# Half-size loads, nine slots, and one value unit split unevenly over the DMA engines, in a one-token attention block

## The chip, the cores and the metric

The kernel runs on one core of a Trainium2 chip. The metric is the device time of one execution in microseconds; lower is better. The kernel before takes 393.2 us (median of three runs, 392.14 to 393.55).

## The reference

One token (x, 1024 numbers) goes through two blocks, and a scalar gate mixes them. Block A is attention against a long cache: 32 query heads share 4 key/value groups, the cache holds 65,536 positions of 128 numbers for each group. Block B is a gated mixer for a sequence of one.

```
q = (x @ wq) as 32 heads of 128
scores = q . k_cache / sqrt(128)            # 32 x 65536, 8 heads use one group
a = softmax(scores) @ v_cache @ wo          # 4096 -> 1024
z = gelu(x @ w_in)                          # 1024 -> 3584 = z1 (1792), z2 (1792)
b = (z1 * (w_sp * layernorm(z2) + b_sp)) @ w_out
g = sigmoid(sum(x * gate_w))
out = g * a + (1 - g) * b
```

All inputs are bf16. Keys and values are 67.1 MB each, wq and wo 8.4 MB each, w_in 7.3 MB, w_out 3.7 MB: 162 MB that are read once.

## The kernel before

Every operation is given to a recorder (`R.op`, short `P`) with its engine, what it reads and what it writes. The recorder derives the waits between engines from that and emits each engine's instructions in the order in which they were given. A transfer has a semaphore of its own name that rises by 16, one for each DMA engine that has finished its part.

The caches are worked through in units of 8192 positions (`UK`): 8 units a group, 32 in all, each 2 MB of keys and 2 MB of values. In a unit, partition p holds 64 consecutive positions, 16 KB. Two neighbouring units are loaded by one transfer (`pair`, `kv`), 32 KB a partition.

All large inputs go through one ring in SBUF of `NS` = 5 slots of 32 KB a partition (`SLOT` = 16384 elements). `load` writes the order down in a list, `stream`; `issue(upto)` gives SP the transfers in this order (L338), round robin over the slots. The first five are issued at once (`issue(NS)`). After that, `done(key)` is called where PE has used a unit; when the last unit of a load is done, the load five places later is issued. SP waits in order. The order of the list is: query weights (two loads), then key pairs with the mixer's input weights (`win`, two loads) and output weights (`wout`, one) between them, then key pairs and value pairs in turn with values nine units behind, then the attention's output weights (`wo`, four loads of 16 KB a partition).

Four small transfers are issued by ACT at the very start (`small`, L261): x and the gate's weights, as 128 partitions with two runs of four numbers each, and two scalars that are broadcast.

PE's order is: the gate's sum (L371, which waits for x and the gate's weights), the queries (L386), and then step by step. A step has up to one key unit n and one value unit n - 9. For the key unit PE transposes 64 tiles of 128x128 in eight batches (`k_piece`, L411); ACT (L416) and DVE (L419) bring each batch from PSUM to one of `NKTS` = 6 buffers; PE multiplies them with the queries (`s_piece`, L433) and DVE takes the scores to one of `NSC` = 10 buffers with their maximum (L438). For the value unit ACT takes exponentials (L459), PE turns them (L466), DVE copies (L469) and PE multiplies them with the values (`pv_piece`, L478). Values start nine units late because the group's maximum must be known. The mixer's two matrices are worked in between: `win_piece` (L526) after key units 1 and 3, two parts each, `wout_piece` (L574) after key unit 6. At the end PE multiplies the attention output with `wo` (L621), DVE adds both blocks (L627), and SP stores 2 KB (L630).

## Time and profile before

| What | Value |
|---|---|
| Median of three runs | 393.2 us |
| The profiled execution's own time | 393.2 us |
| Its span in the profile | 390.4 us |
| Busy share PE / PE weight load / DVE / ACT | 70% / 50% / 41% / 32% |
| Bulk DMA queue q1, share of 16 engines | 97.1%, 162.01 MB |
| Rate over the span | 415 GB/s read |
| Granted TensorE clock, mean | 0.85 |
| Landing of x and of the gate's weights, after issue | 22.4 and 39.2 us |
| Median from issue to landing, key and value pairs | 30.2 and 31.7 us |

How to read it. The page cuts the span into 40 slices of 9.8 us and gives for each the busy tenths of every engine, of the 16 DMA engines together (DMA) and their rate (GB/s). Queue q1 carries the transfers that SP issues, q10 those of ACT; q8 and q14 carry instructions and tables that the engines' sequencers fetch. The chain that ended last goes back from the last instruction to what released it. An answer by windows has one line for each stretch: start and end, length, busy time and number of instructions of PE, PE weight load, DVE, ACT and POOL, granted clock, DMA share, GB/s. The trace also keeps every DMA packet (queue, bytes, start, duration, but not which of the 16 engines carried it) and the time of every semaphore step of a transfer.

### The profile page before, as it was taken

To read this page: it belongs to the slowest core of one execution; us is meant where nothing else is said; L and a number is where in the kernel's file an instruction comes from. 1 tells how busy PE (TensorE), PEld (TensorE's weight loads), DVE (VectorE), ACT (ScalarE), POOL (GpSimd) and SP (SyncE) were. 2 spreads that over 40 slices of the span, in tenths; PEclk is the share of its full clock that TensorE was granted. 3 is DMA by queue.
4 is the path that set the end of the run, shared out by engine and by line. 5 is a ranking of instruction groups with operands and counts; after the bars stand their busy time and mean duration, and the time that the engine had idled before them with its cause. 6 is when DMAs were issued, how large, how long until landed. Compare 5 with 4: busy or idle time off the path is not lost.

```text
span 390.4 us, 8502 instructions
## 1 busy us (share of the span) xinstructions
PE 274.1 (70%) x3902; PEld 194.6 (50%) x3902; DVE 160.2 (41%) x347; ACT 124.4 (32%) x171; POOL 1.5 (0%) x8
## 2 busy tenths in 40 slices
PE   0000699996999899976787596957974959574552
PEld 0000678885776676745565474645743736221121
DVE  2000043435666666644664263536742636410020
ACT  1000033332556555551355151613551425231000
POOL 1000000000000000000000000000000000000000
PEclk9999998685999999996899598968995989856555
DMA  8999999999999999999999999999999999999992
GB/s 322 430 430 437 418 412 441 426 428 425 411 405 431 433 426 431 428 431 428 427 431 428 428 431 430 425 435 435 428 431 433 428 426 431 433 431 421 416 415 96
DMA packets 6778, 162.54 MB, mean 416 GB/s; under 512 B 1492, under 2 KB 1496, under 8 KB 1496
## 3 DMA queue, kind: packets, MB, share of 16 engines
q1 hardware_dynamic: 5912, 162.01, 97.1%
q8 instruction: 30, 0.49, 0.5%
q10 hardware_dynamic: 832, 0.00, 0.1%
q14 instruction: 4, 0.03, 0.0%
HBM read 162.01 MB, written 0.00 MB: 415 GB/s over the span
## 4 chain that ended last, share of the span: by engine, by line
DMA 55%; PE 36%; DVE 6%; issue 1%; ACT 1%; ACTq 0%; DVEq 0%
DMA arena<-in_A_k_cache_dram 31%; PE pb L411 18%; DMA arena<-in_gate_w_dram 10%; DMA arena<-in_A_v_cache_dram 8%; PE pb L433 6%; DMA arena<-in_A_wo_dram 6%; PE pb L526 3%; DVE arena L419 3%; PE pb L478 3%; PE pb L386 2%; DVE arena L438 2%; PE pb L466 1%; ACT arena L416 0%; PE pb L621 0%; PE pb L574 0%
## 5 line engine op out<-in xcount | busy, mean ns | idle before, releaser
L411 PE MATMUL pb<-arena 128*128 128x128 bf16 x2048 | 153.6, 235 | 31.7 <-DMA arena<-in_A_k_cache_dram 31.7
L411 PEld LDWEIGHTS pb<-arena 128*128 128x128 bf16 x2048 | 131.9, 106 | 60.1 <-DMA arena<-in_A_k_cache_dram 34.7
L419 DVE COPY arena<-pb 128x1024 bf16<-128x1024 bf16 x160 | 108.3, 689 | 111.2 <-PE pb L411 110.2
L416 ACT ACTIVATE arena<-pb 128x1024 bf16<-128x1024 bf16 x96 | 98.0, 1021 | 162.2 <-PE pb L411 162.2
L433 PE MATMUL pb<-arena 128*32 128x512 bf16 x512 | 55.0, 420 | 6.1 <-DVE arena L438 4.2
L478 PE MATMUL pb<-arena 128*32 128x512 bf16 x512 | 39.9, 440 | 14.5 <-DMA arena<-in_A_v_cache_dram 10.5
L371 PE MATMUL pb<-arena 128*128 128x1 f32 x2 | 0.6, 362 | 41.0 <-DVE arena L370 41.0
L478 PEld LDWEIGHTS pb<-arena 128*32 128x32 bf16 x512 | 14.0, 104 | 28.5 <-issue 13.5
L459 ACT ACTIVATE arena<-arena 128x512 bf16<-128x512 f32 x32 | 22.8, 713 | 14.3 <-PE pb L466 12.6
L469 DVE COPY arena<-pb 128x512 bf16<-128x512 bf16 x32 | 13.6, 424 | 28.4 <-PE pb L466 28.4
L433 PEld LDWEIGHTS pb<-arena 128*32 128x32 bf16 x512 | 13.3, 93 | 22.9 <-DVE arena L438 7.7
L438 DVE TENSOR_SCALAR_CACHE_REDUCE arena<-pb 128x512 f32<-128x512 f32 x32 | 21.8, 682 | 2.8 <-PE pb L433 2.8
L371 PEld LDWEIGHTS pb<-arena 128*128 128x128 f32 x2 | 0.5, 313 | 41.0 <-DVE arena L370 41.0
L369 DVE TENSOR_TENSOR arena<-arena 128x8 f32<-128x8 bf16 x1 | 0.2, 168 | 37.2 <-DMA arena<-in_gate_w_dram 37.2
L466 PE MATMUL pb<-arena 128*128 128x128 bf16 x128 | 14.8, 248 | 0.0
L466 PEld LDWEIGHTS pb<-arena 128*128 128x128 bf16 x128 | 8.7, 109 | 11.4 <-issue 10.6
L526 PEld LDWEIGHTS pb<-arena 128*128 128x128 bf16 x224 | 13.6, 158 | 0.5 <-issue 0.5
L526 PE MATMUL pb<-arena 128*128 128x1 bf16 x224 | 13.8, 198 | 0.0
L373 ACT ACTIVATE arena<-pb 128x1 f32<-128x1 f32 x1 | 0.2, 171 | 37.0 <-PE pb L371 37.0
L621 PE MATMUL pb<-arena 128*1 128x256 bf16 x128 | 6.5, 379 | 6.8 <-DMA arena<-in_A_wo_dram 6.8
L386 PE MATMUL pb<-arena 128*128 128x1 bf16 x256 | 7.1, 165 | 2.1 <-issue 2.1
L621 PEld LDWEIGHTS pb<-arena 128*1 128x1 bf16 x128 | 3.6, 108 | 9.4 <-issue 4.4
(78 smaller groups left out, 59.7 us busy)
## 6 DMA issues: line engine op xcount, KB each, us to landing
arena<-in_A_k_cache_dram SPq DMA_DIRECT2D x16, 4096.0 KB, 30.2
arena<-in_A_v_cache_dram SPq DMA_DIRECT2D x16, 4096.0 KB, 31.7
arena<-in_A_wq_dram SPq DMA_DIRECT2D x2, 4096.0 KB, 17.4
arena<-in_A_wo_dram SPq DMA_DIRECT2D x4, 2048.0 KB, 30.1
arena<-in_B_w_in_dram SPq DMA_DIRECT2D x2, 3584.0 KB, 28.0
arena<-in_B_w_out_dram SPq DMA_DIRECT2D x1, 3584.0 KB, 17.3
arena<-in_A_x_dram ACTq DMA_DIRECT2D x1, 2.0 KB, 22.4
arena<-in_gate_w_dram ACTq DMA_DIRECT2D x1, 2.0 KB, 39.2
```

The source lines that it names most:

```text
L386: ins = e.matmul(pf(OB)[:, h:h + 1], sl[:, WQ_N * k + 128 * h:WQ_N * k + 128 * (h + 1)], xT[:, 2 * i + k:2 * i + k + 1], start=(i == 0 and ...
L411: ins = e.transpose(pbf(pb)[:, 128 * t:128 * (t + 1)], sl[:, 128 * (8 * b + t):128 * (8 * b + t + 1)], idb)
L416: P("ACT", lambda e, i=i, pb=pb: e.activation(ktb(i), pbf(pb), ACTF.Copy), w=[("kt", i % NKTS), B(pb)])
L419: P("DVE", lambda e, i=i, pb=pb: e.tensor_copy(ktb(i), pbf(pb)), w=[("kt", i % NKTS), B(pb)])
L433: ins = e.matmul(pf(SCB)[32 * cg:32 * (cg + 1), :], qpad[:, 128 * g + 32 * j:128 * g + 32 * (j + 1)], src, start=(j == 0), stop=(j == 3), ...
L438: P("DVE", lambda e: e.tensor_scalar(scs(n), pf(SCB), 0.0, None, op0=ALU.add, op1=ALU.max, accum_out=maxc[:, n:n + 1]), w=[("sc", n % NSC) ...
L459: P("ACT", lambda e: e.activation(psb(n), scs(n), ACTF.Exp, bias=gcol(g, K_NB), scale=SCALE, accum_out=lp[:, n:n + 1]), r=[("sc", n % NSC) ...
L466: ins = e.transpose(pbf(PTB)[:, 128 * xi:128 * (xi + 1)], psb(n)[:, 128 * xi:128 * (xi + 1)], idb)
L469: P("DVE", lambda e: e.tensor_copy(ptsb(n), pbf(PTB)[:, 0:512]), w=[("ptsb", n % 2), B(PTB)])
L478: ins = e.matmul(pf(OB)[32 * cg:32 * (cg + 1), :], ptsb(n)[:, 128 * xi + 32 * cg:128 * xi + 32 * (cg + 1)], vw(sl, 128 * (4 * cg + xi), [[ ...
L526: ins = e.matmul(pf(MB)[:, z:z + 1], vw(sl, c0, [[FC, 128]]), xT[:, 2 * i + k:2 * i + k + 1], start=(i == 0 and k == 0 and z == 0), stop=( ...
L621: ins = e.matmul(pf(FB)[32 * q:32 * q + 1, 0:QW], ovec[:, 8 * i + c:8 * i + c + 1], sl[:, DO * c + QW * q:DO * c + QW * (q + 1)], start=(i ...
```

## The change

- Every large load is one unit: 2 MB of keys, values, query weights or output weights, 14 KB a partition for `win` and `wout`. The ring has nine slots of 16 KB a partition in place of five of 32 KB, and a load is issued when the one nine places before it is done.
- `win` and `wout` come in four and two loads; their parts are worked after key units 0, 1, 2, 3 and 5, 7. The hidden numbers are placed so that PE's weight reads in `win_piece` step by 7 elements rather than 14. The rows of the query and mixer weights that a partition holds change with it, and so x and the gate's weights come as four runs of two numbers for each partition.
- `NKTS` is 8 and `NSC` is 12.
- One value unit, number 16 (`BAL`), is loaded by two transfers. The first takes partitions 0 to 79; its source is described as 8 groups of 10 rows, which spreads it over 8 DMA engines. The second takes partitions 80 to 127 in the usual way, over all 16, three rows each. The slot's semaphore rises by 32 for it.

## The prediction

> **What bounds the kernel now.** I read the page's slices first, then the DMA queues, the chain that ended last, and last the raw DMA records of the trace.

> ```profile
> span 390.4 us, 8502 instructions
> ...
> PE 274.1 (70%) x3902; PEld 194.6 (50%) x3902; DVE 160.2 (41%) x347; ACT 124.4 (32%) x171; POOL 1.5 (0%) x8
> ...
> DMA  8999999999999999999999999999999999999992
> GB/s 322 430 430 437 418 412 441 426 428 425 411 405 431 433 426 431 428 431 428 427 431 428 428 431 430 425 435 435 428 431 433 428 426 431 433 431 421 416 415 96
> ...
> q1 hardware_dynamic: 5912, 162.01, 97.1%
> q8 instruction: 30, 0.49, 0.5%
> q10 hardware_dynamic: 832, 0.00, 0.1%
> q14 instruction: 4, 0.03, 0.0%
> ```

> No compute engine is above 70%; the sixteen DMA engines are busy from the first slice to the last but one, 97.1% of the span with the bulk queue alone. So the time is the start, the bytes at the DMA rate, and a tail. The chain in order of time shows the tail and one place near the front where the DMA was not the limit:

> ```profile
> 1.21 39.23 DMA arena<-in_gate_w_dram
> 40.96 0.59 PE pb L371 x2
> ...
> 361.59 24.22 DMA arena<-in_A_wo_dram
> 385.95 1.91 PE pb L621 x32
> 387.88 0.42 DVE arena L627
> ```

> PE does nothing before the gate row lands at 40.4, then is behind until about 153. That costs time only if a slot of the ring comes free too late. It does once, in the stretches from 106 to 112:

> ```profile
> 104.00:106.00 2.00, 2.00 (x31) 1.44 (x32) 1.20 (x2) 0.97 (x2) 0.00 (x0) 1.00 1.08 459
> 106.00:108.00 2.00, 2.00 (x37) 1.56 (x34) 1.08 (x2) 1.45 (x2) 0.00 (x0) 1.00 0.95 328
> 108.00:110.00 2.00, 1.79 (x27) 1.16 (x27) 2.00 (x5) 1.02 (x1) 0.00 (x0) 1.00 0.87 344
> 110.00:112.00 2.00, 2.00 (x34) 1.67 (x34) 0.92 (x3) 1.00 (x1) 0.00 (x0) 1.00 0.83 360
> 112.00:116.00 4.00, 4.00 (x97) 3.04 (x95) 1.83 (x4) 1.43 (x3) 0.00 (x0) 1.00 1.08 463
> ```

> (Last two columns: DMA share and GB/s.) SP issued that load at 106.72, when key unit 5 was done; the first engine had run dry at 107.09.

> Three things come from the records below the page. First, packet durations on the bulk queue: a 32,768-byte row takes 1213 ns (median), a 28,672-byte row 1062, a 16,384-byte row 611. Two halves therefore cost 2 x 611 - 1213 = **9 ns more than one whole row**. The four output-weight loads, whose rows are 16 KB, confirm it: the first engine lands them 4.89 us apart, pairs of units 9.706 apart.

> Second, each load adds to its semaphore once per DMA engine, so its sixteen landings show how far the engines have drifted apart. The first load's lie between 12.7 and 13.4, the last one's between 380.5 and 385.8. **The last engine, not the mean (383.3), sets the end.**

> Third, where the drift comes from. Each of q8's 16 KB instruction packets (30 before the end, one per some 12 us) makes one engine lose a 1.04 us gap and 0.48 us on the next row: 1.5 us. They fall on eight engines in turn, four each: 6 us. Each of q14's four table packets (85, 137, 191 and 316 us) costs about 1.0 us; they fall on two engines of the other eight. The dry queue at 107 wiped out up to 1.4 us of lag of the engines that were ahead. At the end six engines stand at 380.5 to 381.1, two at 382.2 and 383.0, eight at 384.0 to 385.8.

> **The change part by part.** The profiled execution took 393.2 us, which is also the median of the three: 390.4 of span, 2.8 around it.

> *Halved rows.* Per engine, keys, values and query weights have 272 rows of 32 KB and the mixer weights 24 of 28 KB. Each becomes two: 296 x 9 ns = +2.7 us on every engine. Transfers go from 41 to 79 (the split one counts twice), each with a 4-byte semaphore packet of 9 ns: 38 x 9 = +0.34. The spacing above gives the same: 2 x 4.891 - 9.706 = 0.076 us a pair, x 37 = 2.8. Nothing hides it, since the queue is full.

> *The rows of x and the gate* come as 512 runs of 4 bytes each in place of 256 of 8: 64 of these per engine rather than 32, at 9 ns each (their median): +0.3. Their landing decides when PE starts. The 8-byte records follow one another once per big packet (1.2 us apart beside 32 KB rows, 1.06 beside 28 KB), so 64 of them ride on 64 half rows: the four query-weight loads through the second mixer-weight load, landing near 40.5 as before. ACT issues them in 0.45 to 0.5 us each and then idles 37 us until L373, so a longer issue there is covered.

> *Nine slots in place of five double ones.* 18.9 MB in flight instead of 21.0; a unit is issued when the unit nine before it is done, where a pair was issued when its tenth and ninth predecessors were. SP's steady issue is 0.33 us, the split's second part one more; 79 x 0.33 = 26 us in 390, with nothing but later loads queued behind the waits. I rolled the order forward with the trace's unit times (query weight 1.7, key 5.3 to 6.6, mixer weight 3.4 on PE; 4.9 and 4.3 on the DMA; 1.7 from issue to first packet). First ring empty at 46.6, the next load issued at 43.3 and flowing at 45.0: margin 1.6. Key unit 10: margin 0.9. Value unit 1: issued 106.7, wanted 106.2: dry for 0.5 us against 1.4 before. But the engines that end last lost only 0.2 there (108.98 to 118.9 is 9.9), being 1.9 late already. So the end gains 0.2 at most; if gate or PE is 2 us late, some 0.5 is lost.

> *Mixer weights* are read with stride 7 instead of 14. L526's 112 matmuls take 6.83 us (61 ns each), L386's, with contiguous weights, 27 ns. Between those ends PE saves 0 to 7.6 us, before 95 us; the DMA covers it. Larger KT and SC: the waits list names no wait for a free buffer of either. Both nothing.

> *The split.* Ten rows plus three on eight engines, three on the other eight, in place of eight on all: 5 x 0.616 = 3.1 us on to one half and off the other. The trace cannot say which half. Bounds for the end, from the rows above: -3.1 (all late engines relieved, no other limits) to +3.1 (the late ones loaded), plus a conflict of writes that no row shows; at worst each of the ten rows takes double, 6.1 us more.

> No row decides between these ends. The late engines are one fixed set of eight and the ten rows go to one fixed set of eight; I take the two as different sets, and carry the other two answers as rivals with their prices. Then the late ones end at 385.8 + 3.3 - 0.2 - 3.1 = 385.8. The loaded eight: the clean ones 380.5 to 381.1, without the 1.4 wait but with 0.5, plus 3.3, plus 3.1: 386.0 to 386.6. Among them, if the late eight are the other half, are the two table engines, now at 1.4 and 2.2 above the middle of the clean ones with one lag wiped out at 107; two packets each make about 2.1: 386.0 + 2.1, so **388 is the new end, +2.2.** 393.2 + 2.2 = **395.4 us**. Even perfect levelling brings little: the mean of 383.3, plus 3.3, less the 0.6 that the dry ring costs on average (1.4 and 0.2 before, 0.5 and 0 after), is 386.0, the old end.

> [...]

> [...]

> **The rivals.**

> *No relief* (the split rows disturb each other, or do not fall on eight engines as written). For it: nothing in the trace shows two engines writing into the same few partitions. Against: sixteen engines write side by side with no packet slowed. The late eight keep 385.8 + 3.3 - 0.2: 396.3; with conflicts on the loaded engines up to 388 + 6.1, 401.5.

> *Wrong half.* The eight that take the instruction packets get the ten rows: 385.8 + 3.3 - 0.2 + 3.1 = 392.0, so 399.4. No row speaks for either half.

> *Late gate.* If the small runs went at one per 1.2 us whatever the row size, the gate would land near 80 and the ring be dry from 46.6 to 82: about 428. The 1.06 beside the 28 KB rows speaks against it.

> *Not slower.* The table packets fall elsewhere, or cost less beside half rows, so the loaded half has no stragglers: end 385.8 to 386.6, total 393 to 394; it decides as soon as their lag is under about 0.5 us. If instruction packets cost a half-row less too, down to 391. Against it: the one at 373, among 16 KB rows, still cost a gap of 1.15 us and 0.47 on the next row.

> **How the numbers follow.** Forecast case 0.50 (own range 394.2 to 396.6), no relief 0.22, wrong half 0.10, late gate 0.05, not slower 0.13. Range 393.0 to 399.6: it leaves out half of the not-slower case, the late gate, and a third of no relief. The runs shown differ by 0.36%, so half a per cent, 391.2 to 395.2, is about what can be told from no change. Faster 0.07 (half of not slower); same 0.30 (the other half, and nearly half of the forecast case); slower the rest, 0.63.

> **What would show it.** Right: some 4,700 more bulk packets (296 x 16) and 600 more semaphore packets; bulk share still 97%; gate landing 40 to 41; the dip at 107 nearly gone; the last load's landings with the two table engines last, the eight instruction engines 2 us ahead of them. Wrong: landings of the eight loaded engines spread by more than 3 us after the split (conflict); the same eight engines last by 11 us (wrong half); first PE work after 45; rows of 16 KB taking other than 611 ns in the key and value stretches.

## The result, and the profile after

The changed kernel takes 410.4 us (median of four runs, 409.9 to 411.6) against 393.2: a ratio of 1.0447, 95% interval 1.0415 to 1.048. That is 17.2 us slower, far above the range on record.

The page of the kernel after, its span, slices and DMA queues:

```profile
span 408.2 us, 8545 instructions
...
DMA  8999999999999999999999999999999999999970
GB/s 310 418 425 418 429 424 421 427 428 426 422 430 424 426 424 426 426 428 421 426 430 430 421 430 422 207 207 379 429 424 429 426 426 429 423 427 432 422 340 21
...
q1 hardware_dynamic: 11248, 162.01, 96.7%
q8 instruction: 31, 0.51, 0.5%
q10 hardware_dynamic: 1344, 0.00, 0.2%
```

Read the DMA digits first: they are nines through the middle, as before. By busy time nothing has happened. Then read the rate below them. Slices 26 and 27 move 207 GB/s where the others move 425, and slice 28 is still low. The engines were busy all that time and moved half. The slice before the last has also fallen, from 415 to 340, and the last from 96 to 21.

The same by windows (start and end, length, busy time and number of instructions of PE, PE weight load, DVE, ACT, POOL, granted clock, DMA share, GB/s), kernel after:

```profile
250.00:255.00 5.00, 4.77 (x73) 3.71 (x74) 3.79 (x9) 1.74 (x2) 0.00 (x0) 1.00 1.08 426
255.00:260.00 5.00, 2.76 (x37) 1.49 (x34) 2.58 (x8) 1.93 (x4) 0.00 (x0) 0.87 1.02 216
260.00:265.00 5.00, 0.00 (x0) 0.00 (x0) 0.57 (x2) 0.00 (x0) 0.00 (x0) 0.50 1.03 203
265.00:270.00 5.00, 3.93 (x41) 2.97 (x41) 2.22 (x5) 0.68 (x1) 0.00 (x0) 0.61 0.94 177
270.00:275.00 5.00, 2.94 (x48) 2.21 (x44) 2.38 (x5) 2.98 (x5) 0.00 (x0) 1.00 0.97 216
275.00:280.00 5.00, 0.00 (x0) 0.00 (x0) 0.00 (x0) 0.00 (x0) 0.00 (x0) 0.58 1.03 334
280.00:285.00 5.00, 2.69 (x21) 1.22 (x22) 0.34 (x2) 0.20 (x1) 0.00 (x0) 0.50 1.01 429
```

From 255 to 280 the five rates fall short of 427 by 211, 224, 250, 211 and 93 GB/s. Times 5 us and divided by 427, that is 11.6 us of lost DMA time. It begins where the split unit's turn comes: SP issued its two parts at 226.2 and 227.1, and the queue holds some 30 us of work (median from issue to landing 29.7 us for a key load, 37.3 for a value load).

The packet records say what a row did. Between 254 and 262 us a 16 KB row took 1225 ns (median), against 613 over the whole run. And it was so **for every row**, not only for those of the split unit: no 16 KB row that began between 255 and 262 us took under 1,088 ns. The landings of the load just ahead of the split one show the same (sixteen engines, us):

```
load two before the split one   249.9 ... 254.9    spread 5.0
load just before it             254.8 ... 266.0    spread 11.2
```

By 256.3 seven engines had finished that load and turned to the split. The other nine were still in an ordinary load, and still their last rows doubled.

The end, by the chain that ended last, kernel after:

```profile
360.15 43.44 DMA arena<-in_A_wo_dram
403.73 1.91 PE pb L620 x32
405.66 0.43 DVE arena L626
```

The tail behind the last landing is the old one. The last landing moved from 385.8 to 403.6, by 17.8 us, exactly as the span did. The last load's sixteen landings lie between 390.8 and 403.6, with a mean of 397.0; before they lay between 380.5 and 385.8, with a mean of 383.3.

### The profile page after: what moved, and what is told of

Same layout as the page of the kernel before. It is cut to its first block, busy times and chain, and to the rows that moved or that the text cites. A ratio compares the mean times of both kernels' runs of the same rounds, so it can differ in the third digit from the quotient of the medians.

```text
span 408.2 us, 8545 instructions
## 1 busy us (share of the span) xinstructions
PE 275.2 (67%) x3902; PEld 193.7 (47%) x3902; DVE 159.9 (39%) x347; ACT 124.4 (30%) x171; POOL 1.5 (0%) x8
## 3 DMA queue, kind: packets, MB, share of 16 engines
q1 hardware_dynamic: 11248, 162.01, 96.7%
HBM read 162.01 MB, written 0.00 MB: 397 GB/s over the span
## 4 chain that ended last, share of the span: by engine, by line
DMA 50%; PE 36%; DVE 7%; another core or an unknown queue 4%; ACT 1%; issue 1%; ACTq 0%; DVEq 0%
DMA arena<-in_A_k_cache_dram 21%; PE pb L410 19%; DMA arena<-in_A_wo_dram 11%; DMA arena<-in_gate_w_dram 10%; DMA arena<-in_A_v_cache_dram 9%; PE pb L432 7%; DVE arena L418 4%; PE pb L477 3%; PE pb L525 3%; DVE arena L437 2%; PE pb L385 2%; PE pb L465 1%; ACT arena L415 0%; PE pb L620 0%
## 5 line engine op out<-in xcount | busy, mean ns | idle before, releaser
L410 PEld LDWEIGHTS pb<-arena 128*128 128x128 bf16 x2048 | 131.5, 106 | 63.6 <-DMA arena<-in_A_k_cache_dram 40.8
L468 DVE COPY arena<-pb 128x512 bf16<-128x512 bf16 x32 | 13.6, 424 | 29.7 <-PE pb L465 29.6
L620 PE MATMUL pb<-arena 128*1 128x256 bf16 x128 | 7.5, 413 | 10.2 <-DMA arena<-in_A_wo_dram 10.2
L465 PEld LDWEIGHTS pb<-arena 128*128 128x128 bf16 x128 | 8.8, 110 | 11.3 <-issue 11.3
L525 PEld LDWEIGHTS pb<-arena 128*128 128x128 bf16 x224 | 12.3, 153 | 0.9 <-issue 0.9
L525 PE MATMUL pb<-arena 128*128 128x1 bf16 x224 | 12.6, 192 | 0.0
L385 PE MATMUL pb<-arena 128*128 128x1 bf16 x256 | 7.1, 165 | 1.9 <-issue 1.9
## 6 DMA issues: line engine op xcount, KB each, us to landing
arena<-in_A_k_cache_dram SPq DMA_DIRECT2D x32, 2048.0 KB, 29.7
arena<-in_A_v_cache_dram SPq DMA_DIRECT2D x31, 2048.0 KB, 37.3
arena<-in_B_w_out_dram SPq DMA_DIRECT2D x2, 1792.0 KB, 15.3
```

The source lines that it names most:

```text
L385: ins = e.matmul(pf(OB)[:, h:h + 1], sl[:, WQ_N * k + 128 * h:WQ_N * k + 128 * (h + 1)], xT[:, 2 * i + k:2 * i + k + 1], start=(i == 0 and ...
L410: ins = e.transpose(pbf(pb)[:, 128 * t:128 * (t + 1)], sl[:, 128 * (8 * b + t):128 * (8 * b + t + 1)], idb)
L465: ins = e.transpose(pbf(PTB)[:, 128 * xi:128 * (xi + 1)], psb(n)[:, 128 * xi:128 * (xi + 1)], idb)
L468: P("DVE", lambda e: e.tensor_copy(ptsb(n), pbf(PTB)[:, 0:512]), w=[("ptsb", n % 2), B(PTB)])
L525: ins = e.matmul(pf(MB)[:, z:z + 1], vw(sl, c0, [[7, 128]]), xT[:, 2 * i + k:2 * i + k + 1], start=(i == 0 and k == 0 and z == 0), stop=(i ...
L620: ins = e.matmul(pf(FB)[32 * q:32 * q + 1, 0:QW], ovec[:, 8 * i + c:8 * i + c + 1], sl[:, DO * c + QW * q:DO * c + QW * (q + 1)], start=(i ...
```

## The experiments

The theory formed from this profile is called "shared write": the split's transfers send several DMA engines to the same few partitions at once, and that halves the rate. Its rivals: the read addresses do it ("read"), the hand-built transfer over eight engines does it ("form"), or the half rows and the smaller ring do it ("ring"). The edits are against the changed kernel unless another is named.

**Without the split.**

```diff
-    BAL = {("v", 2 * NU)}
+    BAL = set()
```

> The changed kernel with value unit 16 loaded like all others; all else of the change stays. Theory 'shared write' (the split's transfers make several DMA engines write into the same few partitions, and that halves the rate for 22 us) and its rivals 'read' (the split's read addresses do it) and 'form' (the hand-built transfer over 8 engines does it) all put the loss into the split: then this run takes the prediction's sum without the split, 393.2 + 3.3 - 0.2 = 396.3 us (395.5 to 397), and no slice of the profile falls to half rate. Rival 'ring' (half rows and smaller slots cost it): 405 us or more, with the rate low elsewhere.

Measured: 395.1 us, ratio to the kernel before 1.0055 (1.0035 to 1.0075), 2.2 us. That is a little under the range, since the half rows cost less than their sum. "Ring" falls; the split alone costs 410.4 - 395.1 = 15.3 us. (Beside these runs the kernel before took 392.9 and not 393.2, so 2.2 and 15.3 add up to a little more than 17.2.) The same windows of this run, and they are flat:

```profile
250.00:255.00 5.00, 4.83 (x53) 3.88 (x54) 3.32 (x8) 1.02 (x1) 0.00 (x0) 0.67 1.01 426
255.00:260.00 5.00, 3.56 (x52) 2.22 (x49) 2.61 (x7) 2.64 (x4) 0.00 (x0) 0.99 1.02 436
260.00:265.00 5.00, 4.34 (x47) 3.18 (x48) 3.71 (x9) 1.02 (x1) 0.00 (x0) 0.69 1.02 429
```

Its last load lands between 382.0 and 388.6, mean 385.4. So the 17.8 us of span split into three: 2.8 us without the split (388.6 - 385.8), 11.6 us by which the split moves the mean (397.0 - 385.4), which is the area of the dip, and 3.4 us of wider spread (6.6 against 3.2 from the mean to the last engine).

**Two ordinary halves.** No hand-built transfer, no uneven share.

```diff
     def split(e, dst, src):
-        a, b = eights(src[0:HALF, :], dst[0:HALF, :])
-        first = e.add_instruction(
...
-        return [first, e.dma_start(dst[HALF:128, :], src[HALF:128, :])]
+        return [e.dma_start(dst[0:64, :], src[0:64, :]), e.dma_start(dst[64:128, :], src[64:128, :])]
```

> The changed kernel, but unit 16's split is two ordinary loads of partitions 0 to 63 and 64 to 127, each over all 16 engines, four rows per engine: no hand-built transfer, no uneven share, and the same neighbouring reads as an ordinary load. 'Shared write': sixteen engines write into 64 partitions, so the unit runs at about half rate; eight rows of 0.61 us become 1.2: 4.9 us more than the kernel without the split, about 401 us (399 to 404), with row durations near 1.2 us around 255 us. 'Form' and 'read': the same time as without the split, about 396.3 us.

Measured: 404.7 us, ratio 1.0285 (1.0254 to 1.0316): 9.6 us more than without the split, twice what was expected and just above the range. Windows of this run:

```profile
255.00:260.00 5.00, 3.68 (x56) 2.34 (x53) 2.83 (x8) 2.64 (x4) 0.00 (x0) 1.00 1.04 233
260.00:265.00 5.00, 0.61 (x4) 0.34 (x4) 1.36 (x4) 0.00 (x0) 0.00 (x0) 0.56 1.01 213
265.00:270.00 5.00, 4.89 (x42) 3.62 (x43) 2.58 (x5) 1.02 (x1) 0.00 (x0) 0.50 1.03 226
270.00:275.00 5.00, 3.51 (x52) 2.67 (x54) 2.04 (x5) 2.64 (x4) 0.00 (x0) 0.92 0.91 236
```

The rate is halved for some 18 us, although an engine's eight rows of this unit fill only half of that at 1.2 us each. The landings show that an engine goes on at that pace into the next, ordinary load: the first one needs some 9.5 us for its eight rows there. The engines lie 5 us apart when the unit's turn comes, so the first are done and back in ordinary work while the last are still in the halves. Everyone is slow from about the first that enters to the last that leaves.

**Other read addresses, same writes.**

```diff
-        return (bass.AP(tensor=ap_s.tensor, offset=ap_s.offset, ap=[[m * n, 8], [n, m], [1, n]]),
+        return (bass.AP(tensor=ap_s.tensor, offset=ap_s.offset, ap=[[4 * n, 8], [n, m], [1, n]]),
```

> The changed kernel with the same split and the same writes, but the eight groups of the first transfer read rows 4e to 4e + 9 instead of 10e to 10e + 9, so neighbouring engines read 64 KB apart rather than 160 KB. The unit's values in partitions 4 to 79 are thus not the right rows, which changes no amount of work. 'Read': the dip vanishes or changes much, 396 to 402 us. 'Shared write' and 'form': the writes and the form are as in the changed kernel, so 410 us (408.5 to 412) with the same dip of some 22 us at 207 GB/s.

Measured: 411.5 us, ratio 1.0451 (1.0419 to 1.0483), the changed kernel's 1.0447 again. The dip is the same too: 206, 236, 167, 226 and 331 GB/s in the five stretches from 255 to 280. "Read" falls, as far as this spacing can say.

**Clean blocks, then a shared rest.** Nearly as uneven, the same hand-built form, but the hand-built part gives each engine four neighbouring partitions.

```diff
-        a, b = eights(src[0:HALF, :], dst[0:HALF, :])
-        first = e.add_instruction(
...
-        return [first, e.dma_start(dst[HALF:128, :], src[HALF:128, :])]
+        out = []
+        for p in (0, 32):
+            a, b = eights(src[p:p + 32, :], dst[p:p + 32, :])
+            out.append(e.add_instruction(
...
+        return out + [e.dma_start(dst[64:128, :], src[64:128, :])]
```

> The changed kernel, but unit 16 comes as two hand-built transfers of partitions 0 to 31 and 32 to 63 over 8 engines, four neighbouring partitions per engine, and one ordinary load of partitions 64 to 127 over all 16: twelve rows on eight engines and four on the other eight, almost as uneven as 13 and 3, same hand-built form. The hand-built part gives each engine partitions of its own. 'Shared write': only the ordinary part shares, 397 to 402 us, with a shorter dip than the changed kernel's. 'Form': the dip is as long as before or longer (two such transfers), 408 us or more.

Measured: 405.6 us, ratio 1.0315 (1.0285 to 1.0345), between the two ranges, so the time alone decides nothing. The windows do:

```profile
255.00:260.00 5.00, 3.37 (x51) 2.03 (x48) 2.80 (x9) 2.64 (x4) 0.00 (x0) 1.00 1.01 338
260.00:265.00 5.00, 0.85 (x9) 0.69 (x10) 1.09 (x3) 0.00 (x0) 0.00 (x0) 0.63 1.11 193
265.00:270.00 5.00, 5.00 (x58) 3.94 (x55) 3.40 (x7) 1.02 (x1) 0.00 (x0) 0.69 0.91 197
270.00:275.00 5.00, 1.74 (x26) 1.10 (x24) 1.19 (x3) 2.64 (x4) 0.00 (x0) 0.99 1.02 233
```

The first stretch holds the hand-built part and runs at 338; until 258 us most rows still take 611 to 640 ns, as long as few engines have reached the ordinary part of partitions 64 to 127. Only then does everything fall to half and below. My range was too low because I had priced sharing for the rows that share, not for all the others beside them.

**Eight neighbours per engine.** One transfer, all sixteen engines, even share.

```diff
-        m = ap_d.ap[0][1] // 8
-        return (bass.AP(tensor=ap_s.tensor, offset=ap_s.offset, ap=[[m * n, 8], [n, m], [1, n]]),
+        m = ap_d.ap[0][1] // 16
+        return (bass.AP(tensor=ap_s.tensor, offset=ap_s.offset, ap=[[m * n, 16], [n, m], [1, n]]),
...
-        a, b = eights(src[0:HALF, :], dst[0:HALF, :])
+        a, b = eights(src, dst)
```

> The changed kernel, but unit 16 comes as one hand-built transfer over all 16 engines in which each engine takes eight neighbouring partitions: same bytes, rows and even share as an ordinary load, one transfer; only which engine writes which partitions differs. 'Shared write' (engines that write into the same few partitions slow every engine to half rate for as long as one of them does): like the two plain halves, 404.7 us (402 to 407), rows at 1.2 us from 255 on for 15 to 18 us. If it is not the pairing of engine and partitions: as without the split, 395.1 us.

Measured: 404.6 us, ratio 1.0309 (1.0277 to 1.0342), as expected. Windows of this run:

```profile
255.00:260.00 5.00, 4.06 (x60) 2.80 (x58) 2.72 (x7) 2.64 (x4) 0.00 (x0) 0.92 0.99 206
260.00:265.00 5.00, 1.03 (x9) 0.78 (x10) 1.61 (x6) 0.00 (x0) 0.00 (x0) 0.76 1.09 242
265.00:270.00 5.00, 5.00 (x50) 3.73 (x48) 2.77 (x6) 1.02 (x1) 0.00 (x0) 0.56 0.97 213
270.00:275.00 5.00, 3.14 (x54) 2.02 (x51) 1.86 (x4) 2.64 (x4) 0.00 (x0) 1.00 0.94 259
```

The same bytes, the same row size, sixteen engines and eight rows each, as in the ordinary load that the run without the split has in its place, at 426 to 436 GB/s. By the edit each engine has eight neighbouring partitions to itself, and the run takes 9.5 us longer than that one. So "shared write" had the time right, but "the same few partitions" does not describe this load: what the engines share was the author's conjecture and is not shown. The records do not name the engine of a row either; that an ordinary load pairs engines and partitions otherwise is inferred from its rate. The reads differ in the same way, since a row's place in memory goes with its partition; that the reads are not it rests on the run with other read addresses.

**The split elsewhere.**

```diff
-    BAL = {("v", 2 * NU)}
+    BAL = {("k", 0)}
```

> The changed kernel with the same uneven split on key unit 0 in place of value unit 16, at about 23 us, where the engines lie 0.5 us apart and not 5. 'Shared write, and the price is half of the time from the first engine that enters to the last that leaves': the window shrinks from 22.7 us to 13 rows of 1.22 us plus 1, about 17, so the mean loss is 8 us and not 11; with the uneven share about 404 us (402 to 407). If the drift has no part in it: 410 us as with value unit 16.

Measured: 406.7 us, ratio 1.0359 (1.0328 to 1.039). The windows of this run, where the engines are still close together (the sixteen landings of the first load lie 0.5 us apart in the kernel after):

```profile
20.00:25.00 5.00, 0.00 (x0) 0.00 (x0) 0.00 (x0) 0.00 (x0) 0.00 (x0) 1.00 1.09 361
25.00:30.00 5.00, 0.00 (x0) 0.00 (x0) 0.00 (x0) 0.00 (x0) 0.00 (x0) 1.00 0.95 207
30.00:35.00 5.00, 0.00 (x0) 0.00 (x0) 0.00 (x0) 0.00 (x0) 0.00 (x0) 1.00 1.05 220
35.00:40.00 5.00, 0.00 (x0) 0.00 (x0) 0.00 (x0) 0.00 (x0) 0.00 (x0) 1.00 0.95 154
40.00:45.00 5.00, 0.00 (x0) 0.00 (x0) 0.00 (x0) 0.00 (x0) 0.00 (x0) 1.00 1.00 413
```

Some 16 us of dip instead of 23, and 3.7 us less in all than at value unit 16. The mean landing of the last load is 395.1, 9.7 us behind the run without the split, where the split at value unit 16 cost 11.6. That is as expected of a smaller drift, but the place in the stream and the small transfers beside it changed too. All five engine columns are zero here, so no compute engine has a part in it either.

This run also shows the slow ordinary rows without any guess about engines. The load behind the split unit is a mixer weight with rows of 14 KB, which no split has. The 64 of these rows that began between 25 and 35 us took 969 to 1,111 ns; without the split the rows of this load take 535.

**The cost doubled.**

```diff
-    BAL = {("v", 2 * NU)}
+    BAL = {("v", 2 * NU), ("v", 3 * NU)}
```

> The changed kernel with two split units, values 16 and 24: the suspected cost doubled. 'Shared write': a second dip; its engines enter it 13 us apart rather than 5, so it is longer than the first: 410.4 + 15 to 20 = 425 to 430 us. If the first loss were a single event (a queue that overflows once, an instruction that loads once): below 415.

Measured: 428.9 us, ratio 1.0931 (1.089 to 1.0973), 18.4 us more than with one and in the range. So it is no single event. The slices of this run show both dips, and a last one at 20 GB/s while a few engines finish:

```profile
GB/s 323 415 417 421 422 422 429 422 426 432 424 425 425 425 430 425 421 426 430 425 424 432 427 421 226 196 376 427 424 427 426 398 224 228 399 424 427 422 213 20
```

The landings divide it otherwise than expected. Those of the last load have a mean of 408.8 us, 11.8 behind the 397.0 with one split: the second split cost the engines on average as much as the first (11.6), although a load just ahead of it landed over 12.4 us and one ahead of the first over 5.3. The rest of what it adds is spread: the last engine lands 10.3 us behind the mean, 6.6 with one split. A larger drift did not make the loss itself larger here.

**The hand-built form alone.** As the run with clean blocks, but partitions 64 to 127 of the unit are left out.

```diff
-        return out + [e.dma_start(dst[64:128, :], src[64:128, :])]
+        return out
```

> As the run with two hand-built transfers of 32 partitions, but partitions 64 to 127 of value unit 16 are not loaded at all (64 rows, 1 MB less; that half of the unit holds an older unit's numbers). The low eight engines carry eight rows, the other eight none, each engine writes partitions of its own. 'Shared write': no dip at all although the share is as uneven as it can be and the form is hand-built; rows stay at 0.61 us; the engines without rows gain 4.9 us. 'Form' or 'uneven share': a dip of ten us or more, 403 us or more. The sixteen landings of these two transfers are those of the low eight engines alone: if the late engines are all among the other eight, they lie within 1 us of each other and the end falls by about 3 us to 392; if some late ones are among the low eight, two groups 3 to 5 us apart and the end stays at 395.1 us.

Measured: 395.0 us, ratio 1.0041 (1.0022 to 1.006), the same as without the split within the intervals. Windows of this run:

```profile
255.00:260.00 5.00, 2.55 (x37) 1.36 (x34) 2.77 (x8) 1.92 (x4) 0.00 (x0) 0.97 1.02 433
260.00:265.00 5.00, 4.99 (x58) 4.03 (x59) 3.54 (x8) 1.02 (x1) 0.00 (x0) 0.69 1.01 426
```

Eight rows on eight engines and none on the others is as uneven as it gets, and there is no dip. "Form" falls, and so does the uneven share as a cause. "Read" loses more ground: neighbouring engines read 64 KB apart here, as in the run with other read addresses, which has the whole dip. The landings of the two transfers come from the eight engines that carry them (the "low eight" of the expectation) alone: four of them finish the first at 257.3 to 257.6, the others at about 258.4, 259.4, 260.7 and 262.4. So some of the late engines are among the low eight, and the end does not move although the others were spared 4.9 us (eight rows of 0.613). The last load of this run lands at 377.2 to 388.7, without the split at 382.0 to 388.6.

**The half rows alone.** The kernel before, its ring and all, with each double load cut in two along the row.

```diff
+                out = []
                 for c0, src in pieces:
-                    ins = e.dma_start(slot(n)[:, c0:c0 + src.shape[1]], src)
-                return ins
+                    w = src.shape[1]
+                    cut = [(0, w)] if w <= 8192 else [(0, w // 2), (w // 2, w)]
+                    out += [e.dma_start(slot(n)[:, c0 + x:c0 + y], src[:, x:y]) for x, y in cut]
+                return out
```

> The kernel before, ring of five double slots and all, but each double load is issued as two transfers that each take one half of every partition's row: half rows, twice the transfers, nothing else. The term of 9 ns a row and a transfer: 296 x 9 ns and 37 x 9 ns, 3.0 us, so 395.9 us, ratio 1.0076 (1.005 to 1.010). If the rows cost nothing and the 2.2 us of the run without the split come from the ring or the small runs: ratio 1.000.

Measured: 395.0 us, ratio 1.0057 (1.0037 to 1.0078). Its page's span and DMA queue:

```profile
span 393.2 us, 8539 instructions
...
q1 hardware_dynamic: 11240, 162.01, 97.3%
```

The last landing is at 388.6, the figure of the changed kernel without its split. So half rows alone account for everything that the change costs beside the split: 2.2 us by the ratios, 2.8 by the profiled spans. Nine slots of single units, the runs of x and the gate, the other reads of the mixer's weights and the larger buffers together add nothing that can be measured; whether a small gain of one hides a small loss of another, these runs don't tell.

## Why the prediction was wrong

The sign was right and the size was not: +2.2 us forecast, +17.2 measured, outside the range. That the run without the split takes 395.1 us, beside the 395.4 forecast, is a coincidence: the forecast had the split in it.

**The split: the step that failed.** The forecast case put conflicting writes at nothing, since no row showed any. A rival with 0.22 priced them, and bounded them as "at worst each of the ten rows takes double, 6.1 us more", on the loaded engines alone. Two things in that bound were wrong. Rows double on all engines, those in ordinary loads too (1225 ns in the median against 613, none under 1,088). And they do so from about the first engine that enters the split to the last that leaves it, some 23 us with an engine drift of 5 us, not for ten rows. The loss is half of that, 11.6 us on average over the engines, and 3.4 us of spread on top; taking the split away gives back 15.3 us.

The trace of before could not show this, since every large load in it was an ordinary one of 128 partitions. A price bounded from such rows is no bound: they are rows without the mechanism. The range should have let in a loss on all engines, and the rival should have had a larger chance, because no row of before tested it.

The runs show which loads are slow. Two halves of 64 partitions ran at 213 to 236 GB/s and eight neighbours per engine at 206 to 259; blocks of four neighbours on eight engines, with partitions 64 to 127 left out, kept 426 to 433. They show the reach too: in the run with the split on key unit 0 none of the 64 ordinary rows escaped (969 to 1,111 ns against 535). What the engines share is not shown, and neither is why an ordinary load of 128 partitions keeps its rate: the records don't name the engine of a row. That eight neighbours per engine cost 9.5 us and an ordinary load nothing says that the pairing counts, not by what route.

**Relief of the late eight.** "I take the two as different sets" was wrong as well. In the run without the unit's upper half some of the late engines are among the eight that carry the hand-built rows (they finish between 257.3 and 262.4). Even with clean writes the split could hardly have brought the end forward: the other engines were spared 4.9 us there, and the time stayed. That q14's packets are tables was not shown either: the page lists them as "instruction", and the table loads of before (ACT_TABLE_LOAD at 3.26, 90.87 and 124.77 us) are at other times than its packets at 85, 137, 191 and 316.

**Half rows.** Right, with some luck in the term: +3.3 us forecast with the small runs, 2.2 by the ratio and 2.8 in the span measured. The 611 and 1213 ns behind the 9 ns are the commonest durations; the medians over all rows are 613 and 1214, which would give 12 ns and 3.6 us for the rows. The 37 more transfers of the run with half rows cost 2.8 us with all their rows. The page after counts 5,336 more bulk packets, as forecast (4,736 rows and 600 for semaphores).

**Ring and gate.** Right: the gate's weights landed at 40.2, forecast near 40.5, and the ring no longer ran dry near 107: by the packet records the engines were busy all of the time from 104 to 120, where before they fell to 0.52 between 107.0 and 107.5. Without the split the first engine lands its loads 4.9 us apart through that stretch. The late gate did not happen.

**The bound on any gain.** The argument that even perfect levelling would only reach the old end fits: without the split the mean landing is 385.4, forecast 386.0 and the old end 385.8.

## What to carry to other kernels

When a load is cut so that it is no longer 128 partitions in one ordinary transfer, first ask which DMA engine will write which partitions. In this kernel an unlucky pairing slowed every engine for about as long as one was in the cut load: one 2 MB load cost the mean engine 9.7 us with a drift of 0.5 us and 11.6 to 11.8 us with 5 and 12, and left the engines further apart. And a DMA that is busy in every slice can still be at half rate (here 207 GB/s beside some 425, at a digit of nine in both): read the GB/s row beside the busy row.

## What was not expected

One 2 MB load in a stream of 162 MB, 1.3% of the bytes, cost 3.9% of the time (15.3 us). The slowdown reached rows of ordinary loads as well: those of 16 KB went from 613 to some 1,200 ns, those of 14 KB from 535 to some 1,050. By what route it reaches them, the runs don't say. They tell the pairing of engine and partitions from the form, the share and the compute engines; of the reads only the spacing was varied on its own, and in one way.
